# Two attention and MLP layers on one Trainium2 core: the 256 KB loads that end the layers, each cut into four loads over 32 rows with a padded source

## The chip, the cores and the metric

The kernel runs on one core of one Trainium2 chip. The metric is the device time of one execution in microseconds (us). Engines are named as the profile names them: PE (TensorE) for matrix products, PEld for its weight loads, DVE (VectorE), ACT (ScalarE), POOL (GpSimd), and SP (SyncE), which here only issues DMAs. A DMA that SP or ACT issues is carried by 16 DMA engines that the whole core shares.

## The reference

One token passes twice through an attention block over a cached context and an MLP, with the same weights and the same cache both times:

```python
def _A_ref(x, k_cache, v_cache, wq, wo):
    q = (x @ wq).reshape(B, Sq, H, Dh) ...
    scores = jnp.einsum("bhqd,bhkd->bhqk", q, k_cache) * (Dh ** -0.5)
    p = _softmax(scores, axis=-1)
    o = jnp.einsum("bhqk,bhkd->bhqd", p, v_cache)
    return o ... @ wo
def _B_ref(x, w1, w2):
    return max(x @ w1, 0) @ w2
x = A_x
x = x + _A_ref(_layernorm(x, axis=-1), A_k_cache, A_v_cache, A_wq, A_wo)
x = x + _B_ref(_layernorm(x, axis=-1), B_w1, B_w2)
x = x + _A_ref(_layernorm(x, axis=-1), A_k_cache, A_v_cache, A_wq, A_wo)
x = x + _B_ref(_layernorm(x, axis=-1), B_w1, B_w2)
```

x has 640 elements, there are 32 heads of 128, the cache holds 8192 positions, and the MLP is 1728 wide. Everything is float32. A head has 4 MB of keys and 4 MB of values, so the cache is 256 MB, and it is read in both layers.

## The kernel before, in words

**The cache in DRAM.** The function `_laid_out` writes keys and values into one flat array `kv`, unit after unit, in the order in which layer 0 uses them. A unit is what one DMA loads: a list of pieces of one head's keys or values, laid out as 128 rows (one for each SBUF partition) that follow each other without a gap. `UNITS` (L41 to L54) says how each head is cut. Most heads are `WHOLE`: one unit of keys and one of values, 4096 KB each. The heads at the ends of the layers are cut finer. Heads 0 and 31 have two units of keys of 2048 KB and the values as `LAST` (L40): 2048 KB, 1024 KB, 768 KB and 256 KB. Counted from zero, the 256 KB unit is unit 5 of its head, the last row of values in the last block: 512 floats, 2 KB, in each of 128 rows.

**The ring.** The units land in one SBUF tile, `ring`, of 128 partitions by 8 * 3496 floats (14 MB). `todo` (L98 to L102) lists the loads in the order in which they are to be issued: all units of heads 0 to 31 for layer 0, then for layer 1 the units of heads 31 down to 0 without those that are still in the ring (`kept`: head 31 and the last units of head 30). Four units of layer 1 are taken from that list and loaded into tiles of their own (`load_beside`, L143). So unit 5 of head 31 is loaded once, as the last load of layer 0, and unit 5 of head 0 is loaded twice: as the sixth load into the ring at the start, and as the last load of layer 1.

**Who issues.** `pump` (L123) walks along `todo`: it looks for room in the ring (`place`), issues the DMA on SP's queue (L133), and notes the place of every piece. It is called at the start and each time that a piece has been used and is released (`release`, L158). SP issues in order, so a load that waits for room, or for the semaphore that it is to count on, holds up all that stands behind it on SP. Semaphores, waits and the order on each engine are made by the framework from the order of the program; a matmul waits until the load that it reads has landed.

**The work on a head.** `scores` (L361) multiplies a piece of keys with the query (L366), `exponentials` and `turn` make the weights of the softmax (L378, L385, L393), and `values` (L420) multiplies pieces of values with them (L427): for each piece and each of four groups `g` one matmul, which reads all 128 rows of the piece. So the matmuls of the 256 KB unit need the whole unit. `output` (L439) closes the head. Chores such as the projection of earlier heads, the queries of later ones and the weight products for the MLP go between the pieces on PE. After the last head `mlp` (L772) follows at once; in layer 0 it leads into layer 1, whose first heads work on what was kept in the ring and on the tiles loaded beside, while SP starts to fill the ring anew.

**Other queues.** ACT's queue loads the projection weights `wq_t` and `wo_t` group by group and the MLP weights once. Instruction code is fetched by DMAs too; the profile lists these as queues of the kind "instruction".

Of the kernel before, what the change touches and what calls it, by code (L numbers as in the profile page):

```python
# [15 lines left out]
P = 128  # L16
D = 640
H = 32
SK = 8192
# [21 lines left out]
UNITS = {h: WHOLE for h in range(H)}  # L41
# [18 lines left out]
LEAD_AT = [range(15, 29), ()]  # L60


def wide(kind, piece):

    return 4 * piece[2] * (1 if kind == "k" else DH) // 8


def size(unit):
    return sum(wide(unit[0], piece) for piece in unit[1])
# [10 lines left out]
def decode_kernel(ctx: ExitStack, tc: tile.TileContext, x, kv, wq, wo, w1, w2, out):  # L80
    nc = tc.nc
# [12 lines left out]
    ring = consts.tile([P, 8 * RING], F32, name="ring")  # L94
# [8 lines left out]
    dram_at, o = {}, 0  # L103
    for h, i in order:
        dram_at[h, i] = o
        o += 8 * P * size(UNITS[h][i])
    live = {}
    at_of = {}

    def place(layer, n):  # L110


        step = max(m for m in (8, 256, 512) if n % m == 0)
        low, high = (0, RING) if layer else ((3072, RING) if n == RING - 3072 else (0, 3072))
        at, best = low, None
        for a, m in sorted(live.values()) + [(high, 0)]:
            a = min(a, high)
            if a - at >= n and (best is None or a - at < best[1]):
                best = at, a - at
            at = max(at, -(-(a + m) // step) * step)  # L120
        return None if best is None else best[0]

    def pump():  # L123
        while todo:
            layer, u = todo[0]
            kind, pieces = unit = UNITS[u[0]][u[1]]
            n = size(unit)
            at = place(layer, n)
            if at is None:
                return  # L130
            todo.pop(0)
            o = dram_at[u]
            nc.sync.dma_start(  # L133
                ring[:, 8 * at : 8 * (at + n)],
                kv[o : o + 8 * P * n].rearrange("(p m) -> p m", p=P),
            )
            for t, piece in enumerate(pieces):
                m = wide(kind, piece)
                live[layer, u, t] = at, m
                at_of[layer, u, t] = ring, 8 * at  # L140
                at += m

    def load_beside(i, where, n):  # L143
        (layer, u), at = beside[i], 0
        kind, pieces = UNITS[u[0]][u[1]]
        assert 8 * size(UNITS[u[0]][u[1]]) == n
        nc.sync.dma_start(
            where[:, at : at + n],
            kv[dram_at[u] : dram_at[u] + P * n].rearrange("(p m) -> p m", p=P),
        )  # L150
        for t, piece in enumerate(pieces):
            at_of[layer, u, t] = where, at
            at += 8 * wide(kind, piece)
# [4 lines left out]
    def release(L, u, t):  # L158
        if (L or u not in kept) and at_of[key(L, u, t)][0] is ring:
            del live[key(L, u, t)]  # L160
            pump()
# [23 lines left out]
    nc.sync.dma_start(xr, x)  # L185
    load_wq(0, nc.sync)
    pump()
    load_wo(0, nc.sync)

# [745 lines left out]
def _hidden_rows():  # L935

    b = [[F_AT[g] + j * P + np.arange(P) for g in range(4)] for j in range(F_TILES)]
    rest = [F_AT[g] + np.arange(F_TILES * P, F_ROWS[g]) for g in range(4)]
    blocks = [x for row in b for x in row]
    blocks.append(np.concatenate(rest[:2]))  # L940
    blocks.append(np.concatenate(rest[2:] + [-np.ones(P - len(rest[2]) - len(rest[3]), int)]))
    return blocks


def _laid_out(A_x, A_k_cache, A_v_cache, A_wq, A_wo, B_w1, B_w2):
    k = np.asarray(A_k_cache)[0].reshape(H, 4, 4, RUN, DH).transpose(0, 4, 1, 2, 3)
    v = np.asarray(A_v_cache)[0].reshape(H, 4, 4, NBL, P, DH).transpose(0, 4, 1, 2, 3, 5)
    kv = np.empty(H * P * SK * 2, k.dtype)
    o = 0
    for h in range(H):  # L950
        for kind, pieces in UNITS[h]:
            n = 8 * sum(wide(kind, piece) for piece in pieces)
            block = kv[o : o + P * n].reshape(P, n)
            o += P * n
            a = 0
            for piece in pieces:
                if kind == "k":
                    r, c, m = piece
                    part = k[h, :, :, r, c : c + m]
                else:  # L960
                    b, r, m = piece
                    part = v[h, :, :, r : r + m, b]
                part = part.reshape(P, -1)
                block[:, a : a + part.shape[1]] = part
                a += part.shape[1]
    w2 = np.zeros((P, FB, D), np.asarray(B_w2).dtype)
    for b, f in enumerate(_hidden_rows()):
        w2[f >= 0, b] = np.asarray(B_w2)[f[f >= 0]][:, _COLS]

    wq = np.asarray(A_wq).reshape(NB, P, NG, HG * DH).transpose(2, 1, 0, 3).copy()  # L970
    last = wq[-1].reshape(P, NB, HG, DH)
    wq[-1] = np.concatenate(
        [last[:, :, :-1].reshape(P, -1), last[:, :, -1].reshape(P, -1)], axis=1
    ).reshape(wq[-1].shape)
    return {
        "x": np.repeat(np.asarray(A_x).reshape(D)[_COLS].reshape(4, DR), 32, axis=0),
        "kv": kv,
        "wq": wq.reshape(NG * P, NB * HG * DH),
        "wo": np.asarray(A_wo)[:, _COLS].reshape(NG, HG, DH, D).transpose(0, 2, 1, 3),
        "w1": np.asarray(B_w1).reshape(NB, P, DFF).transpose(1, 0, 2),  # L980
        "w2": w2,
    }
# [24 lines left out]
```

## Time and profile before

| | |
|---|---|
| time, median of 3 runs | 1367.77 us (1365.71 to 1371.56) |
| span of the profiled execution | 1368.2 us |
| moved by DMA in it | 572.70 MB, mean 419 GB/s |
| PE busy | 1006.9 us, 74% of the span |
| DVE, ACT, POOL busy | 182.4, 113.3, 2.9 us |
| granted TensorE clock, mean | 0.807 |

The page's second part cuts the span in 40 slices of 34.2 us. A digit is the busy share in tenths, for DMA the mean share of 16 DMA engines. The chain of waits goes back from the last instruction: at each step to what released it. In a table of stretches each row gives a stretch of time, each engine's busy time with the number of its instructions in brackets, and at the end the granted clock, the DMA share (1 is all 16 engines busy) and the GB/s moved.

### The profile page before, as it was taken

How to read it: one execution, taken by the hardware profiler on the slowest of the kernel's cores; microseconds unless marked ns; L12 is line 12 of the kernel's file. 1: busy time of each engine (PE TensorE's matmuls, PEld its weight loads, DVE VectorE, ACT ScalarE, POOL GpSimd, SP SyncE). 2: the span in 40 equal slices, each digit the busy share in tenths (PEclk: the TensorE clock that was granted, in tenths of full speed). 3: DMA queues.
4: the chain of work that ended last, by engine and by line, in shares of the span. 5: the costliest groups of instructions: out<-in, count | busy, mean ns of one | idle time of the engine just before them, and what ended most of it. 6: DMA issues, size and time to landing. Idle time of an engine off the chain costs nothing.

```text
span 1368.2 us, 16729 instructions
## 1 busy us (share of the span) xinstructions
PE 1006.9 (74%) x7546; PEld 416.1 (30%) x7546; DVE 182.4 (13%) x696; ACT 113.3 (8%) x305; POOL 2.9 (0%) x10
## 2 busy tenths in 40 slices
PE   6564756777787878788798776667777687677668
PEld 2221212323333334343254322222223222222224
DVE  1010100111101101011122101110111111111112
ACT  0000000100111101011001000000001000000000
POOL 0000000000000000000000000000000000000000
PEclk8786777888878878888798778788878787788787
DMA  9999999999999999999979999999999999999994
GB/s 394 431 432 428 430 435 426 431 429 434 427 433 428 428 432 429 433 427 421 424 299 409 431 433 428 429 433 427 434 427 432 430 430 431 432 429 433 428 425 173
DMA packets 29023, 572.70 MB, mean 419 GB/s; under 512 B 3220, under 2 KB 3352, under 8 KB 5656
## 3 DMA queue, kind: packets, MB, share of 16 engines
q1 hardware_dynamic: 24200, 525.27, 89.8%
q10 hardware_dynamic: 4752, 46.37, 8.1%
q8 instruction: 59, 0.97, 0.3%
q14 instruction: 12, 0.10, 0.0%
HBM read 571.62 MB, written 0.00 MB: 418 GB/s over the span
## 4 chain that ended last, share of the span: by engine, by line
DMA 62%; PE 33%; DVE 2%; ACT 1%; issue 1%; SPq 0%; POOLq 0%; POOL 0%; ACTq 0%; DVEq 0%
DMA ring<-in_kv 61%; PE outs L427 12%; PE ps L366 11%; PE pt L393 2%; PE px L506 2%; ACT p L385 1%; DVE h_t L378 1%; DMA wqc<-in_wq 1%; PE px L312 1%; PE pm L413 1%; PE acc L582 1%; PE px L559 1%; PE acc L332 1%; PE pm L453 1%; PE px L551 0%
## 5 line engine op out<-in xcount | busy, mean ns | idle before, releaser
L366 PE MATMUL ps<-ring,spread_q 128*32 128x512 f32 (+2 forms) x2064 | 321.3, 735 | 178.4 <-DMA ring<-in_kv 178.4
L427 PE MATMUL outs<-ring,pT 128*4 128x512 f32 (+2 forms) x2128 | 325.7, 762 | 51.2 <-DMA ring<-in_kv 50.8
L366 PEld LDWEIGHTS ps<-ring,spread_q 128*32 128x32 f32 x2064 | 62.3, 127 | 291.7 <-DMA ring<-in_kv 188.6
L427 PEld LDWEIGHTS outs<-ring,pT 128*4 128x4 f32 x2128 | 57.8, 101 | 253.6 <-issue 192.1
L378 DVE TENSOR_REDUCE h_t<-ps 128x1 f32<-128x512 f32 x64 | 44.2, 691 | 471.4 <-PE ps L366 471.3
L453 PE MATMUL pm<-h_t,p 128*128 128x1 f32 (+1 forms) x512 | 69.9, 258 | 33.4 <-DVE p L444 33.1
L453 PEld LDWEIGHTS pm<-h_t,p 128*128 128x128 f32 x512 | 64.6, 194 | 94.9 <-DVE p L444 92.8
L385 ACT ACTIVATE p<-ps,h_t 128x512 f32<-128x512 f32 x63 | 43.3, 687 | 575.0 <-DVE h_t L378 547.5
L393 PE MATMUL pt<-row_of,p 128*128 128x16 f32 x512 | 69.9, 269 | 22.3 <-ACT p L385 22.2
L393 PEld LDWEIGHTS pt<-row_of,p 128*128 128x128 f32 x512 | 63.8, 196 | 34.2 <-ACT p L385 34.1
L444 DVE COPY p<-outs 128x256 f32<-128x256 f32 x62 | 26.3, 425 | 346.4 <-PE outs L427 346.4
L406 PE MATMUL pm<-ident,h_t 128*128 128x128 f32 x128 | 31.7, 330 | 40.2 <-DVE h_t L378 40.2
L445 ACT COPY p<-outs 128x256 f32<-128x256 f32 x62 | 23.1, 372 | 456.7 <-DVE p L444 456.7
L406 PEld LDWEIGHTS pm<-ident,h_t 128*128 128x128 f32 x128 | 19.4, 191 | 91.0 <-DVE h_t L378 88.4
L506 PE MATMUL px<-w_t,wct 128*128 128x448 f32 (+1 forms) x80 | 45.6, 656 | 0.0
L413 PE MATMUL pm<-h_t 128*128 128x1 f32 x128 | 27.4, 283 | 24.5 <-DVE h_t L410 24.5
L312 PEld LDWEIGHTS px<-wq_t,ln_xc 128*32 128x32 f32 x630 | 27.5, 155 | 17.7 <-issue 15.1
L312 PE MATMUL px<-wq_t,ln_xc 128*32 128x128 f32 x630 | 31.5, 367 | 1.6 <-DMA wq_t<-in_wq 1.6
L413 PEld LDWEIGHTS pm<-h_t 128*128 128x128 f32 x128 | 21.9, 214 | 30.8 <-DVE h_t L410 30.8
L332 PE MATMUL acc<-wo_t,o_cols 128*32 128x160 f32 x496 | 29.5, 395 | 0.0
L332 PEld LDWEIGHTS acc<-wo_t,o_cols 128*32 128x32 f32 x496 | 20.8, 145 | 18.9 <-issue 14.5
L506 PEld LDWEIGHTS px<-w_t,wct 128*128 128x128 f32 x80 | 13.5, 211 | 37.5 <-issue 36.0
(151 smaller groups left out, 350.8 us busy)
## 6 DMA issues: line engine op xcount, KB each, us to landing
ring<-in_kv SPq DMA_DIRECT2D x104, 4096.0 KB, 25.4
ring<-in_kv SPq DMA_DIRECT2D x27, 2048.0 KB, 24.0
ring<-in_kv SPq DMA_DIRECT2D x19, 1024.0 KB, 20.3
wo_t<-in_wo ACTq DMA_DIRECT2D x14, 1280.0 KB, 17.4
wq_t<-in_wq ACTq DMA_DIRECT2D x13, 1280.0 KB, 17.4
w_t<-in_w ACTq DMA_DIRECT2D x1, 4480.0 KB, 25.0
w_t<-in_w ACTq DMA_DIRECT2D x1, 4320.0 KB, 24.6
ring<-in_kv SPq DMA_DIRECT2D x3, 768.0 KB, 27.9
```

Source lines behind the costliest of these rows:

```text
L312: nc.tensor.matmul(pq[32 * j : 32 * j + 32, :DH], xc[:, c : c + 1].to_broadcast([P, 32]), weights_of(g, c, j), start=(c == 0), stop=(c == ...
L332: nc.tensor.matmul(acc[32 * g : 32 * g + 32, :DR], col.to_broadcast([col.shape[0], 32]), wt[:, g * DR : (g + 1) * DR], start=first, stop=last,
L366: nc.tensor.matmul(hd.ps[32 * g : 32 * g + 32, c : c + n], spread_q[:, 3 - r : 35 - r], tile_of[:, at + g * n : at + (g + 1) * n], start=f ...
L378: nc.vector.tensor_reduce(hd.nm, hd.ps, AX.X, ALU.max, negate=True)
L385: nc.scalar.activation(hd.p, hd.ps, AF.Exp, bias=hd.nm, scale=scale, accum_out=hd.l)
L393: nc.tensor.matmul(pt[:, 16 * b : 16 * b + 16], hd.p[:, b * P : (b + 1) * P], row_of.rearrange("p g r -> p (g r)"), start=True, stop=True,)
L406: nc.tensor.matmul(pt[:, :P], hd.nm.to_broadcast([P, P]), ident, start=True, stop=True)
L413: nc.tensor.matmul(pt[:, :1], hd.l.to_broadcast([P, P]), hd.wi, start=True, stop=True)
L427: nc.tensor.matmul((hd.out if r0 < 3 else hd.out_3)[32 * g : 32 * g + 4, r0:r1].rearrange("p r d -> p (r d)"), hd.pT[:, 4 * i : 4 * i + 4] ...
L444: nc.vector.tensor_copy(oc[:, :2], hd.out[:, :2])
L453: nc.tensor.matmul(pt[:, :n], oc[:, r], hd.w[:, r : r + 1].to_broadcast([P, n]), start=(r == 0), stop=(r == 3),)
L506: nc.tensor.matmul(pt[:, :n], wct[:, c], w1_t[:, c, f : f + n], start=(c == 0), stop=(c == NB - 1),)
```

## The change

Two units, (0, 5) and (31, 5), are treated in another way; all others are laid out and loaded as before, with their offsets in `kv` moved by the padding of the units before them.

- In DRAM the 128 rows of such a unit stand as 32 groups of four rows. A group is 4 * 512 floats, followed by a gap of 128 floats (512 bytes) that is never read.
- In place of one DMA over 128 rows `pump` issues four, each over 32 partitions. Its source is a pattern of three dimensions: eight groups (a), four rows in a group (b), 512 floats (m).

```diff
+EIGHTHS = [(0, 5), (31, 5)]
+GAP = 128
+def span(u, n):
+    return P * n + (GAP * P // 4 if u in EIGHTHS else 0)
...
-        o += 8 * P * size(UNITS[h][i])
+        o += span((h, i), 8 * size(UNITS[h][i]))
...
-            nc.sync.dma_start(
-                ring[:, 8 * at : 8 * (at + n)],
-                kv[o : o + 8 * P * n].rearrange("(p m) -> p m", p=P),
-            )
+            whole = kv[o : o + span(u, 8 * n)]
+            if u in EIGHTHS:
+                rows = whole.rearrange("(q a m) -> q a m", q=4, a=8)[:, :, : 4 * 8 * n]
+                for q in range(4):
+                    nc.sync.dma_start(
+                        ring[32 * q : 32 * q + 32, 8 * at : 8 * (at + n)],
+                        rows[q].rearrange("a (b m) -> a b m", b=4),
+                    )
+            else:
+                nc.sync.dma_start(
+                    ring[:, 8 * at : 8 * (at + n)], whole.rearrange("(p m) -> p m", p=P)
+                )
...
-    kv = np.empty(H * P * SK * 2, k.dtype)
+    kv = np.zeros(H * P * SK * 2 + len(EIGHTHS) * GAP * P // 4, k.dtype)
...
+            whole = kv[o : o + span((h, i), n)]
+            o += whole.size
+            if (h, i) in EIGHTHS:
+                whole.reshape(P // 4, -1)[:, : 4 * n] = block.reshape(P // 4, -1)
+            else:
+                whole[:] = block.reshape(-1)
```

The two units are loaded three times in an execution, so three DMAs of 256 KB become twelve of 64 KB. The bytes read, the place in the ring and the matmuls stay the same.

More of the change, by code (lines that the diff above doesn't have):

```diff
@@ L947, in _laid_out @@
     v = np.asarray(A_v_cache)[0].reshape(H, 4, 4, NBL, P, DH).transpose(0, 4, 1, 2, 3, 5)
-    kv = np.empty(H * P * SK * 2, k.dtype)
+    kv = np.zeros(H * P * SK * 2 + len(EIGHTHS) * GAP * P // 4, k.dtype)
     o = 0
     for h in range(H):
-        for kind, pieces in UNITS[h]:
+        for i, (kind, pieces) in enumerate(UNITS[h]):
             n = 8 * sum(wide(kind, piece) for piece in pieces)
-            block = kv[o : o + P * n].reshape(P, n)
-            o += P * n
+            block = np.empty((P, n), k.dtype)
             a = 0
```

## Prediction

> **What bounds the kernel now.** First the page: the span, the row of DMA shares with its rates, the share of the chain of waits, and from the list of DMAs the queue that fetches code and the loads that matter here.
>
> ```profile
> span 1368.2 us, 16729 instructions
> DMA  9999999999999999999979999999999999999994
> GB/s 394 431 432 428 430 435 426 431 429 434 427 433 428 428 432 429 433 427 421 424 299 409 431 433 428 429 433 427 434 427 432 430 430 431 432 429 433 428 425 173
> q8 instruction: 59, 0.97, 0.3%
> DMA 62%; PE 33%; DVE 2%; ACT 1%; issue 1%; SPq 0%; POOLq 0%; POOL 0%; ACTq 0%; DVEq 0%
> ring<-in_kv SPq DMA_DIRECT2D x3, 256.0 KB, 28.2
> xr<-in_x SPq DMA_DIRECT2D x1, 80.0 KB, 1.9
> ```
>
> All 16 DMA engines are busy in all slices but two: the turn from layer 0 to layer 1 (299 GB/s) and the end (173). In between the stream runs at 425 to 435 GB/s, and time is bytes over that rate. The three loads that the change cuts up spend 28.2 us between issue and landing, but they are only the end of a long queue: 256 KB at 430 GB/s are 0.6 us of 16 engines, 16 KB on each.
>
> Next the chain of waits at the two ends of a layer, in order of time (start, duration, what).
>
> ```profile
> 655.02 19.83 DMA ring<-in_kv
> 674.89 3.10 PE ps L366 x16
> ...
> 700.89 1.84 PE outs L427 x32
> 702.73 0.74 PE acc L582 x6
> 703.47 1.73 PE outs L427 x32
> 705.20 0.84 PE pt L293 x2
> ...
> 773.69 24.08 DMA ring<-in_kv
> ...
> 1307.34 24.38 DMA ring<-in_kv
> 1331.76 2.98 PE outs L427 x16
> ...
> 1354.07 1.73 PE outs L427 x32
> ```
>
> The last landing that sets the end of layer 0 is the one at 674.85, the middle of the keys of head 30. From there to 773.69 the chain is PE with its small partners, through the last head, the MLP and the first heads of layer 1. In layer 1 the chain leaves DMA for good at 1331.72. So neither of the two last loads stands on the chain, though that of layer 0 is close to it, as the third view shows: stretches around the ends of the two streams (the last two columns are the DMA share and GB/s).
>
> ```profile
> 690.00:697.00 7.00, 6.49 (x81) 3.74 (x84) 0.88 (x5) 0.00 (x0) 0.00 (x0) 1.00 0.97 410
> 697.00:699.00 2.00, 2.00 (x21) 1.01 (x14) 0.69 (x1) 0.77 (x2) 0.00 (x0) 1.00 0.89 348
> 699.00:701.00 2.00, 1.62 (x16) 1.44 (x19) 0.65 (x4) 0.31 (x2) 0.00 (x0) 1.00 0.55 228
> 701.00:702.60 1.60, 1.60 (x36) 0.80 (x32) 0.39 (x2) 0.00 (x0) 0.00 (x0) 1.00 0.52 210
> 702.60:704.20 1.60, 1.60 (x36) 0.75 (x28) 0.00 (x0) 0.00 (x0) 0.00 (x0) 1.00 0.34 133
> 704.20:708.00 3.80, 3.55 (x44) 2.09 (x38) 0.91 (x3) 0.00 (x0) 0.00 (x0) 1.00 0.03 8
> ...
> 1338.00:1345.00 7.00, 6.40 (x48) 2.62 (x44) 0.72 (x4) 0.00 (x0) 0.00 (x0) 0.50 0.99 415
> 1345.50:1347.00 1.50, 1.50 (x20) 0.60 (x15) 0.00 (x0) 0.00 (x0) 0.00 (x0) 0.80 0.62 259
> 1347.00:1350.00 3.00, 3.00 (x33) 1.57 (x24) 0.76 (x2) 0.78 (x2) 0.00 (x0) 1.00 0.51 211
> 1350.00:1351.60 1.60, 1.22 (x13) 1.04 (x16) 0.58 (x4) 0.29 (x1) 0.00 (x0) 1.00 0.17 67
> 1351.60:1353.00 1.40, 1.40 (x28) 0.60 (x24) 0.39 (x2) 0.00 (x0) 0.00 (x0) 1.00 0.00 0
> ```
>
> The reader is to see that the engines don't end together. At the end of layer 0 the share falls within 2 us from 0.97 to 0.55, stays there for 3.6 us, and is 0 soon after 704.2; in layer 1 it stands at 0.51 for 3 us. So about eight of the 16 engines are some 5 us ahead of the other eight, and a load has landed only when its slowest engine is done. The fetches of code account for that: 59 blocks in 0.3% of 16 spans are 0.3% of 21 891 us, 66 us, so 1.1 us each; if the 30 of one layer go to eight engines, each of these loses 30 * 1.1 / 8 = 4.1 us. Which eight they are no view tells, for packets carry no engine's number.
>
> **The change part by part.** It takes away three loads of 256 KB, adds twelve of 64 KB with the same bytes in the same place of the queue, and moves what each DMA engine carries.
>
> *Issuing.* Rows of SP: its issues at the end of layer 0 and after, the durations at L133, and what it waits for in all.
>
> ```profile
> 671.02 4.17 SPq L133 DMA_DIRECT2D ring<-in_kv  x4
> 694.17 0.33 SPq L147 DMA_DIRECT2D wqc<-in_kv  x1
> 1365.64 0.64 SPq L924 DMA_DIRECT2D out<-xr  x1
> L133 SPq DMA_DIRECT2D ring<-in_kv x18: 327/328/435, 644.1 to 718.8; - x18
> L133 SPq EVENT_SEMAPHORE  x16: 17/17/28, 644.0 to 719.2; - x16
> SPq L133 <- DMA ring<-in_kv: 444.7, 117, 12.3
> ```
>
> Nine more issues of 0.33 us are 3.0 us of SP in all (5.8 us if each takes the 0.64 us of the store of four rows). SP waits 444.7 us for landings alone, and after the last issue at 675.2 it stands still until 694.17. What it might delay are its next issues: up to three of the four can wait for earlier loads to give a semaphore free. A row of 117 such waits says that this is its daily state; at 430 GB/s the three loads of 2048 KB ahead of them are 4.9 us each, so the fourth would go out about 15 us after 675, at 690, still ahead of the wqc load at 694.17 and of the queue's end at 704.2. Cost: nothing, covered by the queue. Without that cover it would be a dry queue, at 1.9 us (xr) for each load.
>
> *Transfer.* The bytes are the same. A price for each further load in a full queue is bounded by two rows that follow each other:
>
> ```profile
> 655.00:675.00 20.00, 12.05 (x128) 4.94 (x132) 2.39 (x9) 1.45 (x4) 0.00 (x0) 0.88 1.01 423
> 675.00:690.00 15.00, 13.17 (x68) 5.20 (x68) 2.23 (x8) 1.45 (x4) 0.00 (x0) 0.59 1.01 431
> ```
>
> The first stretch carries the small units of heads 29 and 30 (320 to 2048 KB), some ten loads, the second whole 2048 KB loads. 8 GB/s of 431 over 20 us are 0.4 us, so 0.04 us for a load; at the other end stands a load alone in an empty queue, 1.9 us. I take 0.04, since these loads stand in a full queue: six more on the path of layer 0, 0.2 us.
>
> [...]
>
> *Which engines.* Here the trace of before has no row: all its loads into the ring are over 128 rows. The source's outermost dimension now counts eight, so I take it that a load is shared by eight engines, and that it is the same eight for all four. They then carry 32 KB of a unit in place of 16 KB, 0.6 us more, and the other eight carry nothing, 0.6 us less. Two such units are in layer 0, one at its start and one at its end. If the eight are those that are ahead, the lagging ones save 0.6 us before 674.85 and everything that hangs on them comes 0.6 us sooner; the second unit is then no longer the last to land, which brings nothing, because the 768 KB load ahead of it still comes at the lagging engines' pace. If they are the lagging ones, or some of these, 674.85 comes 0.6 us later, and the last load 1.2 us later. How much of that PE sees, its weight loads tell:
>
> ```profile
> 704.45 0.13 PEld L427 LDWEIGHTS outs<-ring,pT 128*4 128x4 f32 x4 [0.19 <-issue]
> 704.77 0.13 PEld L427 LDWEIGHTS outs<-ring,pT 128*4 128x4 f32 x4 [0.19 <-issue]
> ```
>
> These are the eight of the last piece. They would come at 705.05 with the delay of 0.6, and the data at about 704.2 + 1.2 = 705.4: 0.35 us of waiting. Ends: -0.6 and +1.0 us. In layer 1 the last data come at 1351.6 and their matmuls are the last quarter of the 1.73 us from 1354.07, so 3.8 us of cover hide 0.6; without it they would cost that. At the start PE's matmuls of head 0 are 40 in a row, and the load that they release goes out with a queue of 30 us ahead of it:
>
> ```profile
> 27.28 5.95 PE outs L427 x40
> 33.25 30.23 DMA ring<-in_kv
> ```
>
> *Waiting for four semaphores.* The first matmul of the last piece needs four loads in place of one: three more waits, by SP's row 17 to 28 ns each, 0.05 to 0.08 us at the end of each layer, 0.1 us together. Behind them on PE stand the closing of the head and the MLP, all on the chain, so this counts in full.
>
> *Sum.* 0 (issue) + 0.2 (loads) + 0.1 (waits) + (-0.6 to +1.0) = -0.3 to +1.3 us on the profiled 1368.2. Two of three arrangements (the eight lag; the eight are mixed) lie at the upper end, one at the lower; I take +0.5. The span stands 0.4 us above the median of the runs, so on that scale I predict 1367.8 + 0.5 = 1368.3 us: a change that can't be told from none. About 0.5%, 6.8 us, is what a measurement of this kernel can tell from no change; its three runs alone lie 5.9 us apart.
>
> **The rivals.**
>
> *One after the other* (slower). If the four loads wait for one another, because they write the same columns of one tile or for want of a free semaphore, the queue is dry behind the first. Each of the three that follow costs a round of 1.9 us, 5.7 us in all: once at the start, where SP's later loads stand behind them, once at 704.2, where PE has 0.3 us of cover, so 5.4, and once at 1351.6, where 3.8 are covered, so 1.9. Sum 13.0: 1381. It decides as soon as one round is longer than what is queued ahead. For it: SP's issues are in order, and landings hold it 117 times. Against: the rows lie in different partitions, and nothing in the program needs an order.
>
> *Overhead* (slower, at the border). If each load costs 0.3 us of its own plus a fixed part as when xr goes alone (1.9 us less the 0.2 us of its 80 KB), halved by overlap with its neighbours, 0.85 us, then a unit takes 4 * 0.85 = 3.4 us in place of 0.6, twice on the path of layer 0: +5.6 us, and in layer 1 under cover: 1373.4. [...] Against it: the 0.04 us above.
>
> *Fewer engines* (slower). If four engines carry a unit, 64 KB each, that is 2.4 us, +1.8 at two places: 1371.4. If one, 9.7 us, +9.1 at two places: 1386. Against: eight is the outermost count on the source's side and 32 on the other.
>
> [...]
>
> *The lag goes* (faster). If PE's close of the layers did hang on the last load, and it landed with the engines that are ahead, about 699 in place of 704.2 and 1346 in place of 1351.6, up to 5.2 us would be won at each end: 1357. Against: the 768 KB load before it still needs all 16.
>
> *It doesn't do what it says.* If the 32 rows are still shared by all 16 engines, 2 rows each, only 0.3 us remain: 1368.1, inside the forecast.
>
> **How the numbers follow.** Forecast, with the last rival in it: 0.72, own range 1364 to 1372 from the spread of the runs around 1368.3. One after the other 0.09, overhead 0.07, fewer engines 0.04, the lag goes 0.08. Within 0.5%: 0.72 + 0.03 (half of overhead) + 0.01 (four engines) = 0.76; faster 0.08; slower the rest, 0.16. The range 1363 to 1376 takes in the forecast, overhead and four engines, and leaves out 0.09 + 0.08 + 0.02 = 0.19.
>
> **What would show it.** Twelve loads of 64 KB in the list of DMAs, no wait of PE over 0.5 us at the last piece, and the chain leaving DMA near 674 and 1332. For the eight that are ahead: a DMA share near 0.5 for a shorter time after 699; for the lagging eight: for a longer time. Wrong: a digit under 9 in the first slices, issues of L133 2 us apart at the end, or a landing of the small loads far behind 704 on the chain.

## The result, and the profile after

| | before | after |
|---|---|---|
| median of the runs, us | 1367.82 (1365.71 to 1371.56, 10 runs) | 1371.27 (1369.20 to 1374.35, 10 runs) |
| after over before | | 1.0024, 95% interval 1.0015 to 1.0032 |
| span of the profiled execution, us | 1368.2 | 1370.5 |
| granted TensorE clock, mean | 0.807 | 0.803 |

The change makes the kernel slower by 3.3 us, with an interval of 2.1 to 4.4 us (0.0015 and 0.0032 of 1367.8). That is inside the 0.5% that the prediction called no change and inside its range; but ten runs of each are enough to tell it from nothing, so "a change that can't be told from none" didn't hold. The granted clock isn't the reason: its mean over the ten runs after is 0.806, and 0.806 to 0.807 over the runs of the kernel before on the three later occasions. The run of which the second profile was taken lasted 1372.28 us, 1.8 us more than its span.

The page of the kernel after, the same rows as before, and from its list of DMAs the new loads:

```profile
span 1370.5 us, 16744 instructions
DMA  9999999999999999999979999999999999999993
GB/s 385 430 432 434 426 435 428 427 431 431 430 428 433 427 433 430 428 430 419 425 288 414 432 431 429 430 432 429 433 429 431 429 430 427 433 429 432 429 424 161
q8 instruction: 59, 0.97, 0.3%
DMA 69%; PE 28%; DVE 2%; ACT 1%; issue 1%; SPq 0%; POOLq 0%; POOL 0%; ACTq 0%; DVEq 0%
ring<-in_kv SPq DMA_DIRECT2D x12, 64.0 KB
```

The stream in the middle runs at the same rate. The slices that hold the three small units are the ones that fell: the first (394 to 385 GB/s), the turn of the layers (299 to 288) and the last (173 to 161). The row of the small loads has no time to landing, for a reason that is given under "Which engines" below.

The table of stretches, at the same places as before:

```profile
697.00:699.00 2.00, 2.00 (x28) 0.87 (x21) 0.63 (x1) 0.00 (x0) 0.00 (x0) 1.00 0.91 371
699.00:701.00 2.00, 2.00 (x20) 1.23 (x10) 0.35 (x2) 1.07 (x3) 0.00 (x0) 1.00 0.83 280
701.00:702.60 1.60, 1.22 (x19) 0.72 (x22) 0.75 (x4) 0.00 (x0) 0.00 (x0) 1.00 0.57 218
702.60:704.20 1.60, 1.60 (x34) 0.69 (x28) 0.00 (x0) 0.00 (x0) 0.00 (x0) 1.00 0.34 132
704.20:706.40 2.20, 1.71 (x28) 0.50 (x21) 0.42 (x1) 0.00 (x0) 0.00 (x0) 1.00 0.13 52
...
1347.00:1350.00 3.00, 3.00 (x24) 1.51 (x20) 0.21 (x1) 0.00 (x0) 0.00 (x0) 0.62 0.62 217
1350.00:1351.60 1.60, 1.60 (x18) 0.73 (x10) 0.48 (x1) 0.78 (x2) 0.00 (x0) 1.00 0.43 175
1351.60:1353.90 2.30, 1.92 (x23) 1.37 (x25) 1.04 (x5) 0.29 (x1) 0.00 (x0) 1.00 0.09 33
```

Both ends of the queue lie later. Between 699 and 701 the share is 0.83 where it was 0.55, so the engines that were ahead are busy longer; and between 704.2 and 706.4, where the queue of the kernel before was all but empty (0.03 from 704.2 to 708), there is still 0.13, two engines' worth. In layer 1 the share at 1350 to 1351.6 is 0.43 where it was 0.17.

What PE makes of it, first after, then before (timeline of PE; in brackets the idle time ahead of the instruction and who ended it):

```profile
701.75 1.91 PE L444 MATMUL outs<-ring,pT 128*4 128x384 f32 x32
703.47 0.92 PE L599 MATMUL acc<-w_t,ln_xc 128*32 128x448 f32 x8
704.18 1.72 PE L444 MATMUL outs<-ring,pT 128*4 128x384 f32 x24
706.43 0.40 PE L444 MATMUL outs<-ring,pT 128*4 128x128 f32 x8 [0.52 <-DMA ring<-in_kv]
706.76 0.91 PE L310 MATMUL pt<-w_t,ident 128*128 128x384 f32 x2
```

```profile
700.83 1.91 PE L427 MATMUL outs<-ring,pT 128*4 128x384 f32 x32
702.55 0.92 PE L582 MATMUL acc<-w_t,ln_xc 128*32 128x448 f32 x8
703.26 1.94 PE L427 MATMUL outs<-ring,pT 128*4 128x384 f32 x32
705.13 0.91 PE L293 MATMUL pt<-w_t,ident 128*128 128x384 f32 x2
```

Two things make 706.76 of 705.13. The last head starts its values 0.92 us later (701.75 for 700.83), and PE then stands 0.52 us before the last eight matmuls, because the 256 KB unit has not landed; the remaining 0.19 lies in the split block of matmuls. So the wait that the prediction looked for at the last piece is there. The chain of waits shows the same: where it left DMA at 674.85, it now leaves it at 706.34 (690.70 + 15.64), on the last of the four small loads.

```profile
690.70 15.64 DMA ring<-in_kv
708.76 1.00 PE acc L599 x4
...
1315.68 22.46 DMA ring<-in_kv
1338.18 1.14 PE ps L383 x8
...
1353.24 1.84 PE outs L444 x32
1355.82 1.73 PE outs L444 x32
```

In layer 1 the chain leaves DMA at 1338.14 (1315.68 + 22.46), one load later in the queue than before (1331.72), on a 2048 KB load and not on a small one; the last values stand at 1355.82 for 1354.07, 1.75 us later.

**Reading landings engine by engine.** The trace keeps the times at which a load raises its semaphore as it lands: 16 marks for the 256 KB load at the start before (28.99 to 31.09), eight for the first small load in its place after (28.77 to 29.15). Each is read here as one DMA engine that has finished its part. They carry no engine's number, but sorted they show how far the engines lie apart, and from one load to the next, how long a load occupies an engine. The tables in plain fences below are such marks, in us; "first" is the earliest engine's, the others are offsets from it.

### The profile page after: what moved, and what is told of

It reads as the page before. It is cut to its first block, busy times and chain, and to the rows that moved or that the text cites. A ratio compares the mean times of both kernels' runs of the same rounds, so it can differ in the third digit from the quotient of the medians.

```text
span 1370.5 us, 16744 instructions
## 1 busy us (share of the span) xinstructions
PE 1014.9 (74%) x7546; PEld 415.1 (30%) x7546; DVE 182.6 (13%) x696; ACT 113.2 (8%) x305; POOL 2.9 (0%) x10
## 4 chain that ended last, share of the span: by engine, by line
DMA 69%; PE 28%; DVE 2%; ACT 1%; issue 1%; SPq 0%; POOLq 0%; POOL 0%; ACTq 0%; DVEq 0%
DMA ring<-in_kv 68%; PE ps L383 9%; PE outs L444 9%; PE px L523 2%; PE pt L410 1%; DMA wo_t<-in_wo 1%; PE px L329 1%; ACT p L402 1%; PE acc L349 1%; DVE h_t L395 1%; PE px L576 1%; PE acc L599 1%; PE pm L430 1%; PE px L556 0%; PE pm L470 0%
## 5 line engine op out<-in xcount | busy, mean ns | idle before, releaser
L444 PE MATMUL outs<-ring,pT 128*4 128x512 f32 (+2 forms) x2128 | 334.3, 780 | 46.3 <-DMA ring<-in_kv 46.2
L329 PE MATMUL px<-wq_t,ln_xc 128*32 128x128 f32 x630 | 31.3, 367 | 1.4 <-DMA wq_t<-in_wq 1.4
```

The costliest lines, as they stand in the source:

```text
L329: nc.tensor.matmul(pq[32 * j : 32 * j + 32, :DH], xc[:, c : c + 1].to_broadcast([P, 32]), weights_of(g, c, j), start=(c == 0), stop=(c == ...
L444: nc.tensor.matmul((hd.out if r0 < 3 else hd.out_3)[32 * g : 32 * g + 4, r0:r1].rearrange("p r d -> p (r d)"), hd.pT[:, 4 * i : 4 * i + 4] ...
```

## The experiments

Three theories stood at the start. *Engines*: the unit is carried by eight engines, some of them lagging ones, and these fall back. *Loads*: each further load has a price of its own. *Offsets*: the padding moves the DRAM address of everything behind it. All kernels below but the two by columns were made from one form of the change, in which the load reads as follows (with 32 groups in four parts, `each` is 1 and a group is loaded as it is); PARTS, GROUPS, GAP = 4, 8, 128 is the change itself.

```python
each, step = P // (PARTS * GROUPS), P // PARTS
groups = whole.rearrange("(q a m) -> q a m", q=PARTS, a=GROUPS)[:, :, : each * 8 * n]
for q in range(PARTS):
    nc.sync.dma_start(
        ring[step * q : step * q + step, 8 * at : 8 * (at + n)],
        groups[q].rearrange("a (b m) -> a b m", b=each),
    )
```

**Four loads of 32 rows on 16 engines** (four_on_all).

```diff
-PARTS, GROUPS, GAP = 4, 8, 128
+PARTS, GROUPS, GAP = 4, 32, 0
```

> Both units go as four loads over 32 rows, as in the change, but from a source without gaps, whose outermost dimension is 32, so that each load can be shared by all 16 DMA engines. Theory 'engines' (a unit on eight engines makes some of the lagging ones carry 16 KB more, and a load has landed only with its slowest engine): within 0.4 us of before, and the small loads count 16 engines. Rival 'loads' (nine more loads, their issue, their fixed part, and three more waits on PE): nearly the whole of the 3.4 us that the change costs.

Measured: 1370.88 us (12 runs), ratio 1.0023 [1.0013, 1.0032] to the kernel before.

**One load of 128 rows on eight engines** (one_on_eight): eight groups of 16 rows.

```diff
-PARTS, GROUPS, GAP = 4, 8, 128
+PARTS, GROUPS, GAP = 1, 8, 128
```

> Both units go as one load over 128 rows, whose source is eight groups of 16 rows with a gap of 512 bytes behind each: 32 KB on each of eight engines, with no load more than before. Theory 'engines': 2.5 to 3.5 us slower than before, like the change. Rival 'loads': within 0.4 us of before.

Measured: 1371.57 us (9 runs), ratio 1.0024 [1.0013, 1.0034]. As much as the change, without one more load: *loads* isn't the cause by itself. But four_on_all costs as much with all 16 engines: *engines*, as first stated, isn't either.

**The change at one of its two units** (first_only, last_only).

```diff
-EIGHTHS = [(0, 5), (31, 5)]
+EIGHTHS = [(0, 5)]      # first_only; last_only has [(31, 5)]
```

> Only unit 5 of head 0 (loaded at the start of layer 0 and at the end of layer 1) goes as in the change; unit 5 of head 31 as before. Theory 'engines': the stream of layer 0 is 0.6 to 1.2 us late at 674.85, and nothing more is added at 704: 0.6 to 1.5 us slower than before. Rival 'loads': two thirds of the change, 2.3 us. Rival 'offsets' (that nearly all units stand 16 KB further in DRAM, because of the gaps in the unit of head 0): the whole 3.4 us.

> Only unit 5 of head 31 (loaded once, at the end of layer 0) goes as in the change. No unit's offset moves, since it is the last in DRAM. Theory 'engines': the last data of layer 0 come 0.6 us later or a little more, of which PE has 0.3 us of cover, so 0.3 to 1.5 us slower than before. Rival 'loads': a third of the change, 1.1 us. Rival 'offsets': within 0.3 us of before.

Measured: 1369.88 and 1369.38 us (12 runs each), both with ratio 1.0009 [0.9999, 1.0019]. Each alone is less than half of the change by its ratio, and neither interval is free of 1. last_only moves no offset of any other unit, and costs as much as first_only.

**The padding alone** (padded_one): 32 groups of four rows with gaps, in one load of 128 rows on 16 engines.

```diff
-PARTS, GROUPS, GAP = 4, 8, 128
+PARTS, GROUPS, GAP = 1, 32, 128
```

> The units stand in DRAM as in the change (32 groups of four rows with gaps of 512 bytes, though the units after head 0 move by the same 16 KB), but each is loaded by one load over 128 rows, whose source's outermost dimension is 32. Theory 'engines and loads' (16 KB more on lagging engines, or a fixed part for each further load, both on the stream): within 0.5 us of before, since neither is there. Rival 'any other layout or program costs' (offsets, gaps): 2 to 3 us slower.

Measured: 1369.53 us (12 runs), ratio 1.0005 [0.9992, 1.0017]. *Offsets* and gaps cost nothing that can be seen, though the interval reaches up to 2.3 us; four_on_all, which has neither, costs as much as the change.

**Fewer engines** (one_on_four, one_on_two): one load from four groups of 32 rows, and from two of 64.

```diff
-PARTS, GROUPS, GAP = 4, 8, 128
+PARTS, GROUPS, GAP = 1, 4, 128      # one_on_two has 1, 2, 128
```

> Both units go as one load over 128 rows from four groups of 32 rows with gaps: 64 KB on each of four engines, if the outermost dimension sets their number. Two of the eight engines of the change lag. Theory 'engines': if one of these two is among the four, 1.8 us more at the start and at the end of layer 0, 3 to 4 us slower than before; if neither is, all lagging engines save 0.6 us at the start, and the last unit lands ahead of the 768 KB one: within 1 us of before, rather faster. Which it is shows in the four landings of the unit against the 16 of the load before it.

> Both units go as one load over 128 rows from two groups of 64 rows with a gap: 128 KB on each of two engines. Theory 'engines': if one of the two lags, 4.2 us more at the start and at the end of layer 0, 7 to 9 us slower than before; if neither does, the last unit lands 4.9 us behind their earlier work, at about 703, ahead of the 768 KB one: within 1 us of before, rather faster. Rival 'loads': within 0.4 us of before in any case.

Measured: 1371.94 us (12 runs), ratio 1.0018 [1.0006, 1.0031], and 1379.16 us (6 runs), ratio 1.0074 [1.0051, 1.0096]. That is 2.5 us [0.8 to 4.2] where 3 to 4 or under 1 were expected, and 10 us [7 to 13] where 7 to 9 were; *loads*, with its 0.4 us for one_on_two, falls here too. The marks tell that neither cost comes about as *engines* had it: the unit takes 5.3 us on four engines and 7.8 on two, where 2.4 and 4.9 were reckoned.

**A larger dose on eight engines** (more_on_eight): the 768 KB units (0, 4) and (31, 4) too.

```diff
-EIGHTHS = [(0, 5), (31, 5)]
-PARTS, GROUPS, GAP = 4, 8, 128
+EIGHTHS = [(0, 5), (31, 5), (0, 4), (31, 4)]
+PARTS, GROUPS, GAP = 1, 8, 128
```

> As one_on_eight (one load over 128 rows from eight groups of 16), and the 768 KB units (0, 4) and (31, 4) go the same way: 64 KB more on each of eight engines at the start and at the end of layer 0, in place of 16, with no load more than before. Theory 'engines': the 2.4 us of 64 KB at 27 GB/s come twice in the last landing of layer 0, so 4 to 6 us slower than before. Rival 'loads' (or any cost that is the same for each treated load): at most 1 us more than one_on_eight.

Measured: 1394.13 us (6 runs), ratio 1.0174 [1.0148, 1.0200]. Far more than the uneven share of bytes can cost. The stretches at the start tell why, first of the kernel before, then of this one:

```profile
27.00:29.00 2.00, 2.00 (x14) 0.58 (x17) 0.53 (x3) 0.00 (x0) 0.00 (x0) 0.50 1.15 458
29.00:31.00 2.00, 2.00 (x16) 0.32 (x12) 0.00 (x0) 0.00 (x0) 0.00 (x0) 0.50 0.99 420
```

```profile
29.00:31.00 2.00, 2.00 (x16) 0.44 (x12) 0.00 (x0) 0.00 (x0) 0.00 (x0) 0.50 0.99 162
31.00:33.00 2.00, 1.43 (x11) 0.00 (x0) 0.00 (x0) 0.00 (x0) 0.00 (x0) 0.75 1.01 160
33.00:36.00 3.00, 0.00 (x0) 0.00 (x0) 0.00 (x0) 0.00 (x0) 0.00 (x0) 0.90 0.97 161
```

The DMA share is 1 in both: all 16 engines count as busy, and yet they move 160 GB/s where they moved 420. The engines don't lack work; each row takes them longer, the eight that carry the unit and the other eight with them. The landings say how slow: the 768 KB unit follows the load ahead of it after 9.8 us (26.59 to 36.38), 0.61 us for each of its 16 rows of 6 KB on an engine; in the kernel before it takes 1.88 us (26.46 to 28.34), 0.235 for each of eight rows. That is 80 GB/s for the unit, so the other eight engines move no more than that either. With that a new theory was formed, *rows*: what a load costs is settled by which rows its engines write at the same time.

**Four loads by columns** (four_by_columns): as many loads, issues and waits as in the change, but each over all 128 rows and a quarter of the columns.

```diff
-rows = whole.rearrange("(q a m) -> q a m", q=4, a=8)[:, :, : 4 * 8 * n]
+rows = whole.rearrange("(p m) -> p m", p=P)
 for q in range(4):
     nc.sync.dma_start(
-        ring[32 * q : 32 * q + 32, 8 * at : 8 * (at + n)],
-        rows[q].rearrange("a (b m) -> a b m", b=4),
+        ring[:, 8 * at + 2 * n * q : 8 * at + 2 * n * (q + 1)],
+        rows[:, 2 * n * q : 2 * n * (q + 1)],
     )
```

> The two units go as four loads again, but each over all 128 rows and a quarter of the columns (512 bytes of each row), with no gaps. As many loads, issues and waits as in the change, but all 16 engines and all rows in every load. Theory 'rows' (what a load costs is settled by which rows its engines write at the same time: 32 rows in a load give work to eight engines, or to 16 at half their rate, and both come to about 1.3 us for the unit in place of 0.65; the number of loads costs nothing in a full queue): the four loads occupy an engine for 0.16 us each, the last load of layer 0 lands within 0.7 us of before's 704.3, and the ratio is 1.000 to 1.0008. Theory 'loads' (a load more costs about 0.25 us, whatever its form): the ratio is as in the change, 1.0018 to 1.003, and the last landing near 706.

Measured: 1368.17 us (12 runs), ratio 0.9999 [0.9990, 1.0008]. Its last load of layer 0 landed at 705.08, 0.8 us after the 704.29 of before, 0.1 past the bound that was set for it. The ratio is the one that *rows* gave; *loads* falls. The same stretch of time in four kernels, one row each: by columns, the change, four_on_all and one_on_eight.

```profile
29.00:31.00 2.00, 2.00 (x23) 0.47 (x18) 0.00 (x0) 0.00 (x0) 0.00 (x0) 1.00 1.10 437
```

```profile
29.00:31.00 2.00, 2.00 (x12) 0.30 (x8) 0.00 (x0) 0.00 (x0) 0.00 (x0) 0.50 1.11 339
```

```profile
29.00:31.00 2.00, 2.00 (x16) 0.30 (x8) 0.00 (x0) 0.00 (x0) 0.00 (x0) 1.00 1.03 328
```

```profile
29.00:31.00 2.00, 1.82 (x16) 0.11 (x8) 0.00 (x0) 0.00 (x0) 0.00 (x0) 0.72 1.06 251
```

All engines busy in each, but 437, 339, 328 and 251 GB/s: the three that are slower in the runs by 0.23 to 0.24% are those that lose rate here.

**A larger dose in three forms** (more_by_columns, more_on_all, more_in_four): the four units of more_on_eight, by columns, as 32 rows on 16 engines, and as in the change.

```diff
-EIGHTHS = [(0, 5), (31, 5)]
+EIGHTHS = [(0, 5), (31, 5), (0, 4), (31, 4)]
```

> The same four loads by columns, for the 768 KB units (0, 4) and (31, 4) too: 24 loads more than before... of them 12 of 192 KB and 12 of 64 KB in place of six, so 18 more. Theory 'rows': within 1.5 us of before, 1367 to 1370; a 768 KB unit still occupies an engine for 1.9 us. Theory 'loads': 18 loads more at 0.25 us, +4 to +5 us.

> The same four units, each as four loads over 32 rows, no gaps, the source's outermost dimension 32, so that all 16 engines take part with two rows each. Theory 'rows': half rate on all engines; a 768 KB unit occupies an engine for 3.7 to 3.9 us in place of 1.9, so the engines are 2.5 us late after the start and 5 us at the end of layer 0; PE follows with 4 to 5 us, 1372 to 1374. Theory 'loads': as many loads as by columns, so the same +4 to +5 us as there; a difference of over 2 us between this kernel and the one by columns speaks for 'rows'.

> The change itself (four loads over 32 rows, eight groups of four rows with gaps) on the same four units. Theory 'rows': each row group of four goes at full rate (about 84 ns for 2 KB, 234 ns for 6 KB), so eight engines are occupied for 3.7 us by a 768 KB unit and the others not at all; the slowest of the eight are 2.5 us late after the start and 5 us at the end of layer 0, and the time is 1371 to 1374, as on all 16 engines and not 1394 as with one load from eight groups of 16 rows. If the 25 us of that kernel came from eight engines alone, this one is near 1390 as well.

Measured: 1370.01 us (11 runs, ratio 1.0011 [1.0003, 1.0020]), 1377.07 us (5 runs, 1.0062 [1.0050, 1.0074]) and 1379.63 us (8 runs, 1.0082 [1.0053, 1.0111]; they lie between 1374.72 and 1391.70). With the same number of loads the two forms over 32 rows are 7 and 10 us slower than the one by columns, which decides for *rows* against *loads*; by columns it is at the edge of what *rows* gave, 1367 to 1370. Both other sizes lie above what was expected of them, 1372 to 1374 and 1371 to 1374, and the wide scatter of more_in_four wasn't explained. Its profile is of one of the two longest runs (1390.35 us), which are also the two with the lowest granted clock (0.791 and 0.787, the others 0.800 to 0.817). In it the last small load of layer 1 went out only at 1364.26, as an earlier load with its semaphore had landed (1364.25), and landed at 1369.28, where more_on_all has 1361.21; no trace of a short run is there to compare.

By columns too there is a loss of 1.3 us. What goes with it is of another kind (SP's timeline, then a stretch):

```profile
3.81 24.08 SPq L145 DMA_DIRECT2D ring<-in_kv  x8
28.10 2.40 SPq L150 DMA_DIRECT2D ring<-in_kv  x2
```

```profile
29.00:31.00 2.00, 2.00 (x16) 0.39 (x12) 0.00 (x0) 0.00 (x0) 0.00 (x0) 1.00 0.85 183
```

SP's loads count on eight semaphores. In the traces before and after none goes out until the earlier loads on its semaphore have landed (in the change one at 6.81 after 6.79, one at 18.91 after 18.90), so never more than eight are under way. Eight small loads hold them all, and the 2048 KB load behind them goes out only at 28.10, as the first of the small ones has landed (28.08). The 1 MB that is queued lasts 2.4 us, and then the queue is short: 183 GB/s. The 2048 KB load begins to land at 36.12, 2.0 us later than in four_by_columns (34.17). All three kernels of this dose share this; the change, with four small loads at a place, doesn't have it.

## Why the prediction came out as it did

**Issuing cost nothing: right.** SP's row for the small loads, then SP at the end of layer 0:

```profile
L146 SPq DMA_DIRECT2D ring<-in_kv x12: 667/668/853, 4.2 to 1338.2; - x12
```

```profile
672.29 1.28 SPq L151 DMA_DIRECT2D ring<-in_kv  x3
676.03 15.34 SPq L146 DMA_DIRECT2D ring<-in_kv  x4
695.66 0.33 SPq L164 DMA_DIRECT2D wqc<-in_kv  x1
```

An issue takes 0.67 us, the upper of the two prices taken, and the fourth went out at 690.70 where 690 was forecast. The first of the four starts to land at 698.57, so the queue never ran dry behind them, and *one after the other* didn't come in the change.

**A further load, 0.04 us: nearly right.** By columns the unit occupies an engine for 0.86 us (28.49 to 29.35), in place of 0.65 before (28.34 to 28.99): 0.07 us for each of three further loads, smaller rows included.

**Waiting for four semaphores, 0.1 us: not separated.** four_by_columns has the same four waits; the upper end of its interval bounds them, with everything else, at 1.1 us.

**Which engines: the number of engines and the arrangement were right, the size of the term was not.** A load of the change raises its semaphore nine times (the first one at 5.41, as it is issued, and eight times from 28.77 to 29.15), eight of them as an engine lands: there are eight engines, as taken. With four groups there are four landings (one_on_four) and with two there are two (one_on_two). (The profile looks for 16, which is why it has no time to landing for these rows and for some others; the landing at 706.34 on the chain is right by the marks.) Of three arrangements it was the mixed one, as the 1696 KB load shows. It is the landing at 674.85, after which PE ran without waiting for a load (the last unit of the keys of head 30, which the prediction calls their middle):

```
1696 KB, before: first 668.11; 0.00 ... 4.87 4.89 4.94 5.01 5.04 6.20 6.33 6.74
1696 KB, after:  first 668.33; 0.00 ... 4.66 4.73 4.76 4.83 4.94 6.28 7.60 7.68
```

Of the lagging engines two fell about 1 us further back and the rest stayed. Of those ahead, whose offsets the dots leave out, the first two stayed and six fell back: the third to the eighth mark came 0.9 to 1.8 us later than before. So two of the eight are lagging ones, the other six are ahead. The first small load at the end of layer 0 says the same: six of its marks lie between 698.57 and 702.05, the last two at 705.26 and 705.35. For this the prediction had +0.6 us at this landing and +1.2 at the last, and 1.0 us in all as the upper end. Measured in the two profiles were +1.16 (674.85 to 676.01) and +2.05 (704.29 to 706.34). A single execution is no sure measure, so here are the landings of all kernels with one unit treated at each place, those that keep the rate first (the times are medians of the runs, taken on different occasions):

```
                  1696 KB   last of layer 0      time, us
before             674.85        704.29           1367.8
padded_one         675.45        704.88           1369.5
four_by_columns    675.39        705.08           1368.2
after              676.01        706.34           1371.3
four_on_all        675.67        706.35           1370.9
one_on_eight       676.75        707.82           1371.6
first_only         676.38        705.81           1369.9
last_only          675.28        705.66           1369.4
```

Against the mean of the first three (675.23 and 704.75) the change is 0.8 us late at the first landing and 1.6 at the second. first_only is late at both, last_only at the second alone, as it should be.

The step that failed is this sentence: "They then carry 32 KB of a unit in place of 16 KB, 0.6 us more, and the other eight carry nothing, 0.6 us less." It took every engine at its own pace. At the start, where nothing else disturbs, the marks of the change and of the load behind it are:

```
                    before                  after
768 KB       first 28.34             first 28.46
256 KB       first 28.99             first 28.77, 29.09, 29.89, 30.49 (four loads)
2048 KB      first 33.89; most by    first 34.21; seven by 34.44,
             34.68, one at 35.99     nine from 35.26 to 35.77
```

The eight that carry the unit need 2.0 us for it (28.46 to 30.49) in place of 0.65, 1.4 us more and not 0.6; the others, which should be 0.6 us ahead, are no earlier than before (34.21 for 33.89; the ninth late mark is an engine that was 2 us behind already at the 768 KB load). The first two small loads take 0.31 and 0.32 us, half of the 0.65 that an undisturbed engine took before for twice the bytes, but the third and the fourth, over rows 64 to 127, take 0.80 and 0.60. more_in_four shows that this hangs on what the other engines do meanwhile, and not on these rows alone: there the first unit's loads, three times as large and over the same four quarters, land at 27.68, 28.63, 29.55 and 30.53, all at the same pace (0.9 to 1.0 us), while the queue behind them is short (the 2048 KB load, issued at 27.97, lands first at 36.20, so by the 4.9 us that it took before, 28.99 to 33.89, it began near 31.3); then the small ones land at 30.83, 31.19, 31.90 and 32.48, the last two again at 0.71 and 0.58, once the other eight engines have the 2048 KB load to write. So in these two kernels the pace of an engine hung on what the others moved at the same moment, and on the rows: beside the 2048 KB load the first two small loads of the change, over rows 0 to 63, kept theirs (0.31 and 0.32 us). Whether the engines slow each other at the writes into SBUF or at the reads from DRAM was not shown: every row here goes with one place in DRAM, only the gaps move it, and the reads weren't tested apart.

The marks of the other forms give the rates. A load of 64 KB over 32 rows takes 0.32 us on 16 engines (four_on_all, 28.47 to 29.76 for four) and 0.31 on eight (the first two of the change, 28.46 to 29.09). Shared evenly, that is 4 KB and 8 KB on an engine, 13 and 26 GB/s each, where 16 KB in 0.65 us were 25 before. One load of 256 KB takes 2.2 us from eight groups of 16 rows (one_on_eight, 28.45 to 30.67), 118 GB/s; 5.3 us from four groups of 32 (one_on_four, 28.43 to 33.69), 50 GB/s; and 7.8 us from two groups of 64 (one_on_two, 28.45 to 36.23), 34 GB/s. That is 15, 12 and 17 GB/s an engine, and the 80 GB/s of the 768 KB unit of more_on_eight are 10. Why these are so far under 25 was not shown.

**From the landings to the time.** The prediction gave the mixed arrangement +1.3 us and took +0.5; both lie under the lower end of what was measured, 2.1. That the time is inside the range is due to the width of the range, 1363 to 1376, which was to take in two of the rivals, and not to the sum. Two of the prediction's own signs went against it: PE waits 0.52 us at the last piece, where 0.5 was the most, and the chain leaves DMA at 706.34, on a small load, and at 1338.14, where it was to be near 674 and 1332.

The path is in part shown: by columns the chain leaves DMA at 675.39, as before, in four_on_all at 705.69, on the 768 KB load ahead of the small ones, and in one_on_eight at 707.81, on the unit. The size isn't: in the profile PE is 1.6 us late at the end of layer 0 and 1.75 at the end of layer 1, and the runs say 3.3. What lies between wasn't found at a place. Single executions can't show it: padded_one, whose ratio is 1.0005, issues the load into mix, which follows the end of the last head, at 709.99, where before had 708.19 and the change 709.81. In layer 1 the last 2048 KB load but one landed 1.5 us later than before in the change (1343.03 for 1341.51), but 1.3 later by columns (1342.80) and 2.8 in padded_one (1344.30), so the delay there can't be put down to the change.

**Layer 1's cover: right.** The last small load landed at 1353.83; its eight matmuls are the last quarter of 1.73 us from 1355.82, so 3.3 us of cover were left of 3.8, though it came 2.2 us later than before (1351.66) and not 0.6.

**The rivals.** *Overhead*, 0.85 us for a load beside its neighbours: 0.3 to 0.8 were measured, but for want of rate and not as a fixed price, since by columns it is 0.2. (The 0.85 is half of the 1.7 alone; the 0.3 that the prediction names beside it isn't in it.) *Fewer engines*: 1371.4 was forecast for four, and one_on_four has 1371.94, by the forecast number but not by the forecast way, so that is luck; the unit takes 5.3 us there and not 2.4, and why so little of it comes through wasn't looked into. One engine alone wasn't tried. *The lag goes*: no, the 768 KB load still landed at 705.03. *It doesn't do what it says* was priced at 0.3 us for all 16 engines; four_on_all is that kernel, and costs as much as the change (1.0023).

## What to carry to other kernels

Cutting a load by rows wasn't neutral here even in a full queue: ask which rows all engines work on at one moment, for in more_on_eight the DMA share stayed at 0.99 while GB/s fell (162 for 420). If a load must be cut, cut it by columns: four loads over all 128 rows took 0.9999 of the time, four over 32 rows 1.0023 (on 16 engines) and 1.0024 (on eight). And count the loads under way: eight small ones in a row held all the semaphores in more_by_columns, the 2048 KB load behind them went out only at 28.10, and the rate fell to 183 GB/s.

## What was not expected of the hardware

An engine that writes rows of 6 KB took 0.61 us for a row in more_on_eight and 0.235 before, and all 16 engines counted as busy meanwhile, among them eight that had no part in the slow load: the 2048 KB load behind it began to land only at 38.51 where before it was 33.89. An issue of a load that eight engines carry took SP 0.62 to 0.67 us (medians), on four 0.58 and on two 0.56, and one that 16 carry 0.32 to 0.33. Behind a unit on four or two engines the issue of a 2048 KB load took SP up to 6.2 us (one_on_four, 12.15 to 18.30) and 14.1 (one_on_two, 12.09 to 26.20); what held it wasn't looked into.
